# The halves of the gathered experts' weights: VectorE in place of ScalarE and GpSimd, and a two-step maximum in the routing's search

## The chip, the cores and the metric

The kernel runs on one core of a Trainium2 chip. A core has five engines that work side by side, each through its own instructions in order: PE (TensorE, matrix products), DVE (VectorE), ACT (ScalarE), POOL (GpSimd, which here also issues the gathers) and SP (which issues plain transfers). An engine that reaches an instruction whose inputs are not there stands still, and everything behind it on that engine stands too. The metric is the device time of one execution in microseconds (us), the median of three runs.

## The reference

```python
def reference(**kwargs):
    attn_out = _attn_ref(**attn_kwargs)            # 4 batches, 8 heads, 576 tokens, 64 features, window masks
    x = ...reshape(B * S, H * D)                   # 2304 tokens x 512
    x = _moe_ref(x=x, **moe_kwargs)                # greedy: each token to one expert, 288 per expert
    return _moe2_ref(x=x, **moe2_kwargs)           # every expert for every token, weights from 8 balancing rounds

# _moe_ref: logits in falling order; a token goes to the expert unless either is taken
for e in range(E):                                 # E = 8, w1[e] is 512 x 1024, w2[e] is 1024 x 512
    mask = assigned == e
    h = np.maximum(x[mask] @ w1[e], 0.0)
    out[mask] = h @ w2[e]

# _moe2_ref
for e in range(E):
    h = np.maximum(x @ w1[e], 0.0)
    out += P[:, e:e + 1] * (h @ w2[e])
```

## The kernel before

Every fp32 matrix product is made of three fp16 products: each operand is split in a high half and a low half (what the high half leaves over), and high x high, high x low and low x high are summed. So each expert's weights must be split before use. A weight piece is 128 x 1024 fp32; an expert has eight of them, four of the first layer (tiles `w1h`, `w1l`, or `w0h`, `w0l` for the first moe2 expert, whose second layer then uses the names `w1h`, `w1l`) and four of the second (`w2h`, `w2l`).

The program has three stretches: attention (to about 170 us), `stage1` (routing, moe1 and the first moe2 expert together, to about 705 us) and `stage2` (the other seven moe2 experts).

**Routing** (`Router.phase`, L511 on) closes one expert per phase, in eight phases; the phase decides which expert's weights and which tokens moe1 takes next. A phase begins with a search in six steps for a threshold. In a step VectorE compares all token maxima with 32 or 64 candidates (`G`, L548), TensorE counts them (L552, tile `r`), VectorE tests the counts (`ok`, L554), TensorE spreads the answer to all partitions (L557), and VectorE takes the largest candidate that holds (`pen`, L560 and L561), which gives `cur` and the next candidates `x` (L540). Each step needs the one before it.

**The order** is written by hand. `main` in `stage1` emits moe1's and moe2's products per phase, `interleave` puts a piece of routing between them whenever enough nanoseconds of products have been emitted (1.2 times what the piece asks for, 0.8 in phase 1), and `pump` puts a weight piece between them every few products. Nothing is reordered later: what is emitted between two routing operations stands between them on its engine. Only phase 0 has no products beside it; there the first moe2 expert's eight pieces are split, and products of no use (`warm`, L700) run.

**Weights** (`weights`, L702 on): four raw buffers. Piece n is scaled and rounded to its high half by ScalarE (L736). The low half is made in one of two ways: with `pool`, ScalarE scales the raw buffer in place (L738) and GpSimd subtracts (L739); without it, VectorE does both in one instruction (L741). Then piece n+4 is loaded into the same raw buffer. Before, `pool` holds for the first moe2 expert and for the moe1 experts of phases 1 to 7; the moe1 expert of phase 0 goes through VectorE. moe1's weights come by gathers that GpSimd issues (L761: one per piece of the first layer, two per piece of the second), since the expert is only known after the phase; the tokens' gathers (L771) stand in the same queue, and so did the subtractions. The first moe2 expert's pieces and the gate's weights (`load_gate2`) are plain loads in SP's queue.

**Hidden features**: ScalarE writes the high half `hh` (L787), VectorE the low half `hl` (L788); moe1's result goes to `x2h`, `x2l` (L821, L822).

## Time and profile before

| what | us |
|---|---|
| runs: median (lowest to highest) | 1966.06 (1960.57 to 1968.34) |
| the profiled execution: its span, first to last instruction | 1959.4 |
| median of the runs less that span | 6.7 |
| PE busy in the span | 1861.5 |
| DVE busy | 1251.1 |
| ACT busy | 853.1 |
| POOL busy | 502.7 |

The span is what the trace shows, and no time outside it is given for the profiled execution; so the span is the profiled execution's own time here. It lies 6.7 us under the runs' median and 1.2 us under their lowest. A busy PE is not a PE at its peak: the ends of products are modelled, and the granted clock can halve their pace.

### The profile page before, as it was taken

To read this page: it belongs to the slowest core of one execution; us is meant where nothing else is said; L and a number is where in the kernel's file an instruction comes from. 1 tells how busy PE (TensorE), PEld (TensorE's weight loads), DVE (VectorE), ACT (ScalarE), POOL (GpSimd) and SP (SyncE) were. 2 spreads that over 40 slices of the span, in tenths; PEclk is the share of its full clock that TensorE was granted. 3 is DMA by queue.
4 is the path that set the end of the run, shared out by engine and by line. 5 is a ranking of instruction groups with operands and counts; after the bars stand their busy time and mean duration, and the time that the engine had idled before them with its cause. 6 is when DMAs were issued, how large, how long until landed. Compare 5 with 4: busy or idle time off the path is not lost.

```text
span 1959.4 us, 35169 instructions
## 1 busy us (share of the span) xinstructions
PE 1861.5 (95%) x14812; PEld 1283.7 (66%) x14812; DVE 1251.1 (64%) x2428; ACT 853.1 (44%) x1400; POOL 502.7 (26%) x457
## 2 busy tenths in 40 slices
PE   6997699899899999999999999999999999999998
PEld 4775466665676756775776677677657766776775
DVE  5986766666631485577657765855776586658555
ACT  6775454344555332434325442424344253434332
POOL 0684565555565143011002000200110030003101
PEclk7996799999999999999999999999999999999999
DMA  9375443332344020002001100200020020001101
GB/s 218 73 152 142 109 99 88 80 78 80 70 102 137 25 65 1 1 23 65 1 1 48 40 1 1 87 1 1 23 65 1 1 65 23 1 3 42 44 2 54
DMA packets 87071, 103.47 MB, mean 53 GB/s; under 512 B 49888, under 2 KB 63968, under 8 KB 86912
## 3 DMA queue, kind: packets, MB, share of 16 engines
q1 hardware_dynamic: 73328, 57.66, 11.0%
q0 software_dynamic: 12912, 43.48, 8.5%
q8 instruction: 116, 1.90, 0.4%
q14 instruction: 43, 0.35, 0.1%
q10 hardware_dynamic: 672, 0.08, 0.0%
HBM read 88.41 MB, written 9.45 MB: 50 GB/s over the span
## 4 chain that ended last, share of the span: by engine, by line
PE 69%; DVE 16%; issue 7%; ACT 3%; DMA 2%; POOL 2%; SPq 0%; POOLq 0%; DVEq 0%; ACTq 0%
PE mm L911 26%; PE mm L944 23%; PE mm L784 7%; PE mm L818 4%; PE mm L839 4%; DVE h512l L923 2%; DVE pen L561 2%; DVE w2l L895 2%; PE r L552 1%; DVE nm L230 1%; DVE G L548 1%; DMA rawq<-in_q_dram 1%; ACT h512h L922 1%; POOL out_dram L959 1%; DVE r L918 1%
## 5 line engine op out<-in xcount | busy, mean ns | idle before, releaser
L944 PE MATMUL mm<-w2h,h512l 128*128 128x256 f16 x1568 | 427.5, 273 | 6.2 <-DVE h512l L923 5.4
L944 PE MATMUL mm<-w2h,h512h 128*128 128x256 f16 x1568 | 427.3, 273 | 3.2 <-ACT h512h L922 1.4
L944 PE MATMUL mm<-w2l,h512h 128*128 128x256 f16 x1568 | 427.3, 273 | 0.0
L911 PE MATMUL mm<-x2l,w1h 128*128 128x512 f16 (+1 forms) x1120 | 400.7, 358 | 0.0
L911 PE MATMUL mm<-x2h,w1h 128*128 128x512 f16 (+1 forms) x1120 | 400.7, 358 | 0.0
L911 PE MATMUL mm<-x2h,w1l 128*128 128x512 f16 (+1 forms) x1120 | 400.7, 358 | 0.0
L911 PEld LDWEIGHTS <-w1h 128*128 128x128 f16 x2240 | 219.2, 98 | 210.1
L944 PEld LDWEIGHTS <-h512h 128*128 128x128 f16 x3136 | 306.2, 98 | 48.7 <-issue 5.6
L914 ACT ACTIVATE r<-mm 128x512 f32<-128x512 f32 (+1 forms) x280 | 151.9, 546 | 333.4 <-PE mm L911 333.4
L885 POOL TENSOR_TENSOR raw<-raw 128x256 f32<-128x256 f32 x28 | 22.4, 799 | 998.9 <-DMA raw<-in_w2b_dram 950.5
L911 PEld LDWEIGHTS <-w1l 128*128 128x128 f16 x1120 | 109.6, 98 | 108.2
L922 ACT ACTIVATE h512h<-r 128x1024 f16<-128x1024 f32 x112 | 118.4, 1057 | 133.4 <-DVE r L918 133.4
L944 PEld LDWEIGHTS <-h512l 128*128 128x128 f16 x1568 | 153.3, 98 | 27.2 <-DVE h512l L923 9.5
L917 DVE TENSOR_TENSOR S<-r 128x256 f32<-128x256 f32 (+1 forms) x140 | 56.3, 402 | 176.6 <-ACT r L914 174.9
L923 DVE TENSOR_TENSOR h512l<-r,h512h 128x1024 f16<-128x1024 f32 x112 | 143.3, 1279 | 38.2 <-ACT h512h L922 38.1
L788 DVE SCALAR_TENSOR_TENSOR hl<-mm,hh 128x288 f16<-128x288 f32 (+2 forms) x128 | 55.5, 452 | 88.4 <-ACT hh L787 86.8
L923 DVE TENSOR_TENSOR h512l<-S,h512h 128x768 f16<-128x768 f32 x112 | 110.7, 988 | 0.0
L787 ACT ACTIVATE hh<-mm 128x288 f16<-128x288 f32 (+2 forms) x128 | 50.4, 405 | 115.2 <-PE mm L784 114.1
L955 DVE SCALAR_TENSOR_TENSOR acc<-t,P,acc 128x512 f32<-128x512 f32 x126 | 97.3, 772 | 5.1
L784 PE MATMUL mm<-xt,w1h 128*128 128x288 f16 x512 | 98.2, 292 | 2.1 <-ACT xt L801 2.1
L969 DVE TENSOR_TENSOR t<-mm,t 128x256 f32<-128x256 f32 x63 | 26.7, 424 | 107.3 <-ACT t L968 107.3
L922 ACT ACTIVATE h512h<-S 128x768 f16<-128x768 f32 x112 | 92.9, 829 | 5.1 <-DVE S L920 4.6
(254 smaller groups left out, 3516.1 us busy)
## 6 DMA issues: line engine op xcount, KB each, us to landing
raw<-in_w1b_dram SPq DMA_DIRECT2D x32, 512.0 KB, 4.5
raw<-in_w2b_dram SPq DMA_DIRECT2D x32, 512.0 KB, 3.7
rawv<-in_v_dram SPq DMA_DIRECT2D x36, 128.0 KB, 2.8
xd<-xo SPq DMA_DIRECT2D x29, 96.0 KB, 2.0
xd<-rpk SPq DMA_DIRECT2D x11, 96.0 KB, 2.1
rawk<-in_k_dram SPq DMA_DIRECT2D x1, 1024.0 KB
rawq<-in_q_dram SPq DMA_DIRECT2D x1, 1024.0 KB
raw<-in_w2a_dram,widx POOLq DMA_INDIRECT x64
```

Of the source, the lines that this page charges most:

```text
L784: nc.tensor.matmul(p, a[:, k, 128 * f:128 * (f + 1)], rhs(k, b), start=(k == 0 and i == 0), stop=(k == KT - 1 and i == 2))
L787: nc.scalar.activation(h[0][:, f, :n], p, AF.Relu)
L788: nc.vector.scalar_tensor_tensor(h[1][:, f, :n], p, 0.0, h[0][:, f, :n], op0=OP.max, op1=OP.subtract)
L818: nc.tensor.matmul(p, a[:, f, c], b[:, f, :CAP], start=(f == 0 and i == 0), stop=(f == FT - 1 and i == 2))
L839: nc.tensor.matmul(p, a[:, f, c], b[:, f, :], start=(f == 0 and j == 0), stop=(f == FT - 1 and j == 2))
L911: nc.tensor.matmul(p, a[:, k, 128 * f:128 * (f + 1)], self.x2[b][:, k, t0:t0 + n], start=(k == 0 and j == 0), stop=(k == KT - 1 and j == 2))
L914: nc.scalar.activation(c[:, s], p.rearrange("p (s t) -> p s t", s=2), AF.Relu, scale=SH)
L917: V.tensor_add(S[:, 0], a21, a22)
L922: nc.scalar.activation(hq[0][:, i, s, :m], x, AF.Copy)
L923: V.tensor_sub(hq[1][:, i, s, :m], x, hq[0][:, i, s, :m])
L944: nc.tensor.matmul(p, h[u][:, i, a, 128 * i0:128 * (i0 + 1)], w[v][:, i, b, :], start=(q in (1, 7) and i == 0 and j == 0), stop=(q in (2, ...
L955: V.scalar_tensor_tensor(self.acc[:, r, :], x, self.P[:, r, e:e + 1], self.acc[:, r, :], op0=OP.mult, op1=OP.add)
```

## The change

The low halves of the eight pieces of the first moe2 expert, and of the 56 pieces of moe1's experts of phases 1 to 7, are no longer made by a scaling on ScalarE and a subtraction on GpSimd but by one instruction on VectorE, as those of phase 0's expert already were. In the routing's search, one custom VectorE instruction that adds, takes the maximum and accumulates it (it leaves a second instruction that reads the accumulator) becomes a plain addition and a plain maximum over the row. Comments and blank lines aside, that is all; lines behind the split move up by 5, and the new maximum is L562.

```diff
@@ Router.phase
                 V.tensor_scalar(pen, q[:, :T], 0.5, -3e38, op0=OP.is_lt, op1=OP.mult)
-                V.tensor_tensor_reduce(out=pen, in0=pen, in1=c, scale=1.0, scalar=-3e38, op0=OP.add, op1=OP.max,
-                                       accum_out=cur)
+                V.tensor_add(pen, pen, c)
+                V.tensor_reduce(cur, pen, axis=AX.X, op=OP.max)
@@ Moe.weights
-    def weights(self, key, letter, fetch, pool):
+    def weights(self, key, letter, fetch):
...
             nc.scalar.activation(hi, r, AF.Copy, scale=sc[lay])
-            if pool:
-                nc.scalar.activation(r, r, AF.Copy, scale=sc[lay])
-                nc.gpsimd.tensor_sub(lo, r, hi)
-            else:
-                nc.vector.scalar_tensor_tensor(lo, r, sc[lay], hi, op0=OP.mult, op1=OP.subtract)
+            nc.vector.scalar_tensor_tensor(lo, r, sc[lay], hi, op0=OP.mult, op1=OP.subtract)
@@ Moe.stage1
-        w0 = self.weights(("b", 0), "a", self.fetch_static(0), True)
+        w0 = self.weights(("b", 0), "a", self.fetch_static(0))
...
-            w = self.weights(("a", ph), "b", self.fetch_gather(ph), ph > 0)
+            w = self.weights(("a", ph), "b", self.fetch_gather(ph))
```

The first place is VectorE in the search of phase 2, steps three and four. Before, two steps stand there like this:

```order
L554 TENSOR_SCALAR ok<-r,rem 8x32
L560 TENSOR_SCALAR pen<-r 128x32
L561 ISA pen,cur<-pen,x 128x32
L561 ISA cur 128x1
L540 TENSOR_TENSOR x<-thr,cur 128x32
L548 TENSOR_TENSOR G<-m,x 128x288 x2
```

Now the same steps read:

```order
L554 TENSOR_SCALAR ok<-r,rem 8x32
L736 SCALAR_TENSOR_TENSOR w2l<-raw,w2h 128x1024
L560 TENSOR_SCALAR pen<-r 128x32
L561 TENSOR_TENSOR pen<-pen,x 128x32
L562 TENSOR_REDUCE cur<-pen 128x1
L540 TENSOR_TENSOR x<-thr,cur 128x32
L548 TENSOR_TENSOR G<-m,x 128x288 x2
L736 SCALAR_TENSOR_TENSOR w2l<-raw,w2h 128x1024
L554 TENSOR_SCALAR ok<-r,rem 8x32
L736 SCALAR_TENSOR_TENSOR w2l<-raw,w2h 128x1024
```

The low half of a second-layer piece has come between `ok` and `pen`, or between `G` and `ok`, and the custom pair (ISA) is now an addition and a maximum.

The second place is GpSimd's queue over one moe1 expert (phase 2's), from its first gathers to those of the next expert. Before:

```order
L761 DMA raw<-in_w1a_dram,widx 128x1024 x4
L771 DMA xg<-xd,idx 96x1024 x3
L739 TENSOR_TENSOR w1l<-raw,w1h 128x1024
L761 DMA raw<-in_w2a_dram,widx 128x512 x2
...
L739 TENSOR_TENSOR w2l<-raw,w2h 128x1024 x4
L761 DMA raw<-in_w1a_dram,widx 128x1024 x4
```

Now:

```order
L756 DMA raw<-in_w1a_dram,widx 128x1024 x4
L766 DMA xg<-xd,idx 96x1024 x3
L756 DMA raw<-in_w2a_dram,widx 128x512 x8
L756 DMA raw<-in_w1a_dram,widx 128x1024 x4
L766 DMA xg<-xd,idx 96x1024 x3
```

The eight subtractions have left the queue, and only gathers stand in it; a gather into a raw buffer now waits for VectorE's instruction on that buffer.

The third place is VectorE at the end of phase 0, where the first moe1 expert's token list `idx` is made. Before:

```order
L634 SCALAR_TENSOR_TENSOR mask<-zv,mask 128x18
L635 TENSOR_TENSOR L<-L,ng 128x144
L643 COPY s_3660<-r 96x6
L644 SCALAR_TENSOR_TENSOR idx<-s_3660 96x3
L527 TENSOR_REDUCE m<-L 128x18
```

Now:

```order
L635 TENSOR_TENSOR L<-L,ng 128x144
L736 SCALAR_TENSOR_TENSOR w1l<-raw,w1h 128x1024
L643 COPY s_3659<-r 96x6
L644 SCALAR_TENSOR_TENSOR idx<-s_3659 96x3
L736 SCALAR_TENSOR_TENSOR w1l<-raw,w1h 128x1024
L527 TENSOR_REDUCE m<-L 128x18
```

The last two pieces of the first moe2 expert now stand around `idx`, and free the raw buffers that the last two of the first four gathers need.

## Rows read from the trace of the kernel before

**Rows 1.** The page: busy time by engine; the chain that ended last, by line.
```profile
PE 1861.5 (95%) x14812; PEld 1283.7 (66%) x14812; DVE 1251.1 (64%) x2428; ACT 853.1 (44%) x1400; POOL 502.7 (26%) x457
PE mm L911 26%; PE mm L944 23%; PE mm L784 7%; PE mm L818 4%; PE mm L839 4%; DVE h512l L923 2%; DVE pen L561 2%; DVE w2l L895 2%; PE r L552 1%; DVE nm L230 1%; DVE G L548 1%; DMA rawq<-in_q_dram 1%; ACT h512h L922 1%; POOL out_dram L959 1%; DVE r L918 1%
```

**Rows 3.** Groups by line, 165 to 640: busy us, mean ns; idle before.
```profile
L738 ACT ACTIVATE raw<-raw 128x1024 f32<-128x1024 f32 x64 | 67.6, 1057 | 5.6
...
L561 DVE CUSTOM_DVE_ANT_0 pen<-pen,x 128x32 f32<-128x32 f32 x28 | 46.2, 1651 | 1.0
L741 DVE SCALAR_TENSOR_TENSOR w2l<-raw,w2h 128x1024 f16<-128x1024 f32 x4 | 4.9, 1222 | 2.9 <-issue 2.1 <-ACT w2h L736 0.8
L561 DVE DVE_READ_ACCUMULATOR2_ANT cur<- 128x1 f32 x42 | 3.3, 79 | 0.0
L609 DVE TENSOR_TENSOR pos<-pos,r 128x36 f32<-128x36 f32 x8 | 1.5, 192 | 0.3
L582 DVE TENSOR_REDUCE wx<-r 128x1 f32<-128x8 f32 x7 | 1.1, 164 | 3.7 <-PE r L580 3.7
```

**Rows 4.** Timeline of DVE and of POOL, 283 to 345: start, us, instruction.
```profile
290.44 5.49 DVE L561 CUSTOM_DVE_ANT_0 pen<-pen,x 128x32 f32<-128x32 f32 x1
...
287.51 8.37 POOL L739 TENSOR_TENSOR w2l<-raw,w2h 128x1024 f16<-128x1024 f32 x4
```

**Rows 5.** PE's waits, 165 to 720: total us, times, longest us.
```profile
PE r L552 <- DVE G L548: 33.7, 13, 5.3
PE mm L839 <- ACT hh L787: 2.7, 2, 2.4
```

**Rows 6.** Waits of all engines, 262 to 640.
```profile
PE r L552 <- DVE G L548: 21.2, 8, 5.3
ACT w2h L736 <- DMA raw<-in_w2a_dram,widx: 17.8, 13, 3.4
```

**Rows 7.** Waits of all engines, 229 to 262.
```profile
PE r L552 <- DVE G L548: 0.2, 1, 0.2
```

**Rows 8.** Windows from PE's restart behind four waits for L548.
```profile
353.22:358.00 4.78, 4.78 (x39) 3.08 (x39) 2.05 (x9) 0.41 (x1) 0.00 (x0) 0.64 0.00 0
410.44:416.00 5.56, 5.56 (x45) 3.66 (x45) 2.88 (x9) 0.82 (x2) 0.00 (x0) 0.69 0.00 0
467.70:474.00 6.30, 6.29 (x35) 2.50 (x35) 2.60 (x8) 0.00 (x0) 0.00 (x0) 0.59 0.01 3
526.42:532.00 5.58, 5.58 (x36) 2.73 (x36) 3.75 (x12) 0.38 (x1) 0.00 (x0) 0.59 0.01 1
```

**Rows 9.** Windows of stage 1: length; busy us (count) by engine, clock, DMA share, GB/s.
```profile
165.00:225.00 60.00, 39.49 (x355) 20.39 (x353) 39.95 (x101) 25.01 (x30) 28.84 (x18) 0.60 0.45 128
229.00:262.00 33.00, 30.36 (x320) 22.57 (x319) 23.73 (x79) 8.62 (x16) 8.55 (x8) 1.00 0.29 90
262.00:560.00 298.00, 274.21 (x2550) 189.52 (x2548) 188.67 (x515) 137.97 (x206) 164.99 (x119) 0.97 0.35 86
```

**Rows 10.** The chain in order of time, 500 to 720: start, us, what.
```profile
620.63 2.14 POOL w1l L739
...
624.31 3.48 DMA raw<-in_w2a_dram,widx
627.87 1.06 ACT w2h L736
```

**Rows 11.** Timeline of DVE and of POOL, 165 to 285.
```profile
219.90 3.48 DVE L741 SCALAR_TENSOR_TENSOR w1l<-raw,w1h 128x1024 f16<-128x1024 f32 x3
...
215.17 0.93 POOL L771 DMA_INDIRECT xg<-xd,idx  x1 [0.72 <-DVE idx L644]
...
221.37 2.85 POOL L761 DMA_INDIRECT raw<-in_w2a_dram,widx  x1 [2.50 <-DVE w1l L741]
224.52 0.96 POOL L761 DMA_INDIRECT raw<-in_w2a_dram,widx  x1 [0.30 <-issue]
```

## The prediction

> **What bounds the kernel now.** The page first. TensorE is busy 95% of the span, and the chain that ended last runs mostly through its products; but one line that is no product stands high in it, the routing's `pen` on VectorE (L561, 2%, so about 40 us of 1959.4) [rows 1]. It is an instruction on 32 or 64 numbers per partition and should be too small to be seen. Look next at its durations: half of them are 225 ns or less, the longest is 7582 ns [rows 2]. The group of 28 has 46.2 us where 28 of the shortest, 0.191, would have 5.3 [rows 2, 3]; some 41 us are standing still inside the instruction.

> The timeline says on whom. One starts at 290.44 and lasts 5.49 us, to 295.93; GpSimd ran four subtractions of `w2l` back to back from 287.51 for 8.37 us, to 295.88 [rows 4]. VectorE was held until GpSimd's last subtraction was over. Whichever of the two makes it so, the custom instruction or the subtraction, both go: all of GpSimd's subtractions in this stretch come from the line (L739) that the change removes.

> Then the waits, for what this costs TensorE. Between 165 and 720 us TensorE's largest wait is for `G` (L548), the work right behind `pen`: 33.7 us in 13 waits [rows 5]. 21.2 us in 8 of them lie in 262 to 640, where moe1 and moe2 run beside the routing [rows 6], 0.2 us in 229 to 262 [rows 7], and the rest, 33.7 - 21.2 - 0.2 = 12.3 us, in phase 0, where TensorE has only products of no use to do, so that there VectorE's own chain counts and not TensorE's wait. [...] So in stage 1 what ends last is a VectorE that GpSimd holds; in stage 2, two thirds of the span, nothing of the change runs.

> **The change, part by part.**

> *The waits for G go.* With L739 gone GpSimd issues only gathers there. Take 21.2 us [rows 6].

> *The clock behind them.* What a window loses is its length times what is missing from 1: 4.78 x 0.36 = 1.7, 5.56 x 0.31 = 1.7, 6.30 x 0.41 = 2.6, 5.58 x 0.41 = 2.3, together 8.3 us [rows 8]. TensorE waited for `G` just ahead of each and was busy through all of each, so without the waits I expect the clock to stay. Bounds: 0 if something else makes it fall, 8.3 if not. I take 8.3.

> *The late weights.* Where no routing runs any more, a piece comes late: a subtraction on GpSimd from 620.63 for 2.14 us, behind it the gather of the next piece, 3.48 us from 624.31, then ScalarE's high half at 627.87 [rows 10], and `hh` queued behind that on ScalarE makes TensorE wait 2.7 us in two waits [rows 5]. Now the buffer is free after VectorE's 1.22 us in place of 1.06 (L738) and 2.14, and each queue of gathers loses eight subtractions. Take 2.6 of the 2.7.

> *VectorE's new work.* 64 instructions at 1.22 us [rows 3] are 78 us, of which 56 (68 us) lie beside the products. VectorE was busy 188.7 of 298 us in 262 to 560 [rows 9], about 41 of it standing still. Some 45 of the pieces fall in there: 188.7 - 41 + 55 = 203 of roughly 270 us, or 75%. Whether that can be borne is answered by a stretch that already works in the new way: from 229 to 262 VectorE splits four `w2l` pieces of phase 0's expert (L741) between the steps of phase 1's search, is busy 23.7 of 33 us, 72% [rows 9], and TensorE waits 0.2 us for `G` [rows 7]. By that row 56 pieces cost 56 x 0.2 / 4 = 2.8 us; I take 3. The other end is each piece fully exposed, 68 us; the row of the same operations between the same steps is the nearer one, so I stay by it. What covers a piece is the products that stand between one step's answer and the next count; if a piece stands where they don't reach, up to 1.22 us is seen, and `ok`, `pen` and `hl` are queued behind it.

> *ScalarE's work that goes.* 67.6 us of scaling [rows 3]. ScalarE is no bound, but `hh` stood behind it; I count nothing, and this is the reason why I don't count more for the line above.

> *Addition and maximum.* 0.19 (L609) + 0.16 (L582) in place of 0.19 (the shortest L561) + 0.08 (the accumulator's read) [rows 2, 3]: 0.1 us more a step, at most 0.2 with the gaps. 36 steps are hidden behind the products between the steps; without that cover they would be 4 to 7 us. The six of phase 0 are counted there.

> *Phase 0* has no cover. VectorE wins about 11 us of standing (the 12.3 us of TensorE's waits, less about 1 us for the comparisons themselves). It pays 8 x 1.22 = 9.8 us of splits, about 1 us for addition and maximum, and up to two splits, 2.4 us, for the gate's weights, whose load stands in SP's queue behind loads into buffers that VectorE now frees; some 2 to 3 us of all this lie behind TensorE's answers (an estimate: a quarter to a third of each split, since TensorE needs a few tenths to answer). So about 0. But the last two pieces free their raw buffers only around `idx`, the first four gathers of moe1's weights wait for those buffers, and the tokens' gathers, which began at 215.17 [rows 11], wait behind them. Two of the four gathers can start only after the splits at the end: I put the start of moe1 1 us later (0 to 3).

> *The gathers beside VectorE's split.* A gather's issue took 0.96 us, but 2.85 us when it fell under VectorE's three splits from 219.90 on [rows 11]. So each of an expert's 12 gathers of weights may be up to 1.9 us slower to issue; but GpSimd's queue loses eight subtractions of 2.14, 17 us an expert, and the row of TensorE's waits in 229 to 262 holds such gathers already. I count 0. [...]

> **Sum.** 21.2 + 8.3 + 2.6 - 3 - 1 = 28.1 us less than the profiled execution's 1959.4, so a span of 1931. The median of the runs is 6.7 us above that span; the same step down from it gives 1966.1 - 28.1 = **1938 us**.

> **The rivals.** (What a measurement of this kernel can tell from no change is about 0.5%, 9.8 us.)

> *VectorE is late instead.* If an eighth to a quarter of the 68 us is exposed (8 to 17 us), and a wait of the old kind with a low clock behind it comes back once or twice (1.7 to 2.6 each), the gain is 10 to 20: 1946 to 1956. For it speak the places where two splits stand with only `ok` between them ahead of the next answer (2.44 us where the old order had none); against it the 0.2 us of [rows 7].

> *VectorE takes all of it back*: nearly half of the 68 exposed, within 9.8 us of 1966. Against it the same row.

> *Slower: the weights' gathers hold VectorE.* ScalarE already stands for the second layer's gathers, 17.8 us in 13 waits, 1.4 each [rows 6]. Until now only ScalarE stood; now VectorE's low half waits for ScalarE's high half, and the search behind it. If each of the 28 gathered second-layer pieces of phases 1 to 7 is exposed so (28 x 1.4 = 39 us) and four low clocks come back (8.3), the waits are 47 against 32 won: 1966 + 15 = 1981. It decides from about 1.1 us a piece (32 / 28). Against it: the gathers come sooner, since no subtraction stands before them, and the four pieces between 229 and 262 did not do it.

> *More than thought*: VectorE stood some 41 us and TensorE waited only half of that; if the search running earlier also removes waits that are put down to others, another 5 to 8 us: 1930.

> *The change doesn't do what it says*, that is the waits come from something else than the subtraction: the end of the held instruction at 295.93 beside 295.88 makes that unlikely, and both partners go at once; it is in the second rival's chance.

> **Numbers.** Likeliest (gain 20 to 36, 1930 to 1946): 0.62. More: 0.06. VectorE late, gain 10 to 20: 0.17. All taken back: 0.09. Slower: 0.06. Faster by over 0.5%: 0.62 + 0.06 + 0.17 = 0.85; within: 0.09; slower: 0.06. The range for 8 in 10 takes the likeliest, a part of the more, and nearly all of the second: 1927 to 1955.

> **What the next profile would show.** Right: the new addition at about 0.2 us with no long ones; no subtraction in stage 1; TensorE's wait for `G` in 229 to 640 down from 21.4 to a few us; a granted clock of 1.00 there; VectorE at about 75% between 262 and the end of the routing; stage 2 unchanged and only shifted. Wrong: waits for `G` or `ok` behind a split, a VectorE wait for `w2h`, or low clocks at new places. Phase 0 is right if moe1's first product starts within 3 us of where it did.

## The result, and the profile of the changed kernel

The change takes the median from 1967.20 to **1938.39 us** (four runs of each; 1936.58 to 1941.52 against 1960.57 to 1972.14): a ratio of 0.9862, with a 95% interval of 0.9843 to 0.9881 (ratios here are worked out from all the runs; the quotient of the two medians would be 0.9854). Forecast were 1938 and 1927 to 1955. The two profiled executions lie closer together, with spans of 1959.4 and 1939.7, since before's was one of the short ones of its kernel and this is the longest of the four of the changed one (1941.5). What follows from that comes below; first the changed kernel's own views.

The page: busy time by engine, and the chain that ended last by line.

```profile
PE 1859.8 (96%) x14812; PEld 1286.3 (66%) x14812; DVE 1274.3 (66%) x2492; ACT 787.6 (41%) x1336; POOL 373.2 (19%) x393
PE mm L906 26%; PE mm L939 23%; PE mm L779 10%; PE mm L813 4%; PE mm L834 4%; DVE h512l L918 2%; DVE w2l L890 2%; PE r L552 1%; DVE nm L230 1%; DMA rawq<-in_q_dram 1%; DVE ptl L256 1%; DVE r L913 1%; ACT h512h L917 1%; POOL out_dram L954 1%; DVE vh L198 1%
```

Below line 735 names stand five lines earlier than before: moe1's products are L779 (were L784), the split is L736 (was L741). `pen`, which had 2% of the chain [rows 1], is no longer among its lines here. GpSimd has 129.5 us less, ScalarE 65.5 less, VectorE 23.2 more: 64 splits of 1.22 are 78, and over 50 of standing still went.

VectorE's groups by line, 165 to 640 (busy us, mean ns; idle time before them and what ended it):

```profile
L736 DVE SCALAR_TENSOR_TENSOR w1l<-raw,w1h 128x1024 f16<-128x1024 f32 x36 | 43.9, 1221 | 12.6 <-ACT w1h L735 10.9 <-issue 1.0 <-DMA raw<-in_w2a_dram,widx 0.5
L736 DVE SCALAR_TENSOR_TENSOR w2l<-raw,w2h 128x1024 f16<-128x1024 f32 x32 | 39.0, 1220 | 18.3 <-ACT w2h L735 17.2 <-PE mm L779 0.5 <-issue 0.4
L561 DVE TENSOR_TENSOR pen<-pen,x 128x32 f32<-128x32 f32 x28 | 5.4, 192 | 1.0
```

The durations of the addition and of the maximum over the whole run (min/median/max in ns):

```profile
L561 DVE TENSOR_TENSOR pen<-pen,x x35: 191/193/226, 183.8 to 520.1; 128x32 f32<-128x32 f32 x28, 128x64 f32<-128x64 f32 x7
L562 DVE TENSOR_REDUCE cur<-pen x42: 185/186/221, 179.7 to 520.3; 128x1 f32<-128x32 f32 x28, 128x1 f32<-128x64 f32 x14
```

The group of 28 that had 46.2 us [rows 3] has 5.4, and its longest instruction takes 226 ns where it took 7582 [rows 2]. Nothing stands still inside an instruction of the search now: `x` takes 226 ns at most and `G` 759, where they took up to 2080 and 3032. New is VectorE's own wait of 17.2 us for ScalarE's high half of `w2`.

TensorE's waits, 229 to 640 (us in total, times, longest).

```profile
PE mm L779 <- DVE x2l L817: 4.3, 3, 2.4
PE r L557 <- DVE ok L554: 3.3, 5, 1.2
PE r L552 <- issue: 2.3, 3, 1.2
PE mm L779 <- ACT xt L796: 0.9, 1, 0.9
PE r L552 <- DVE G L548: 0.4, 1, 0.4
```

The wait for `G` fell from 21.2 + 0.2 [rows 6, 7] to 0.4, and the 2.7 us for a late `hh` [rows 5] are gone. In their place stand 3.3 us for `ok` (0.9 before), which is queued behind a split.

Windows: length, busy us (count) of TensorE, its weight loads, VectorE, ScalarE and GpSimd, granted clock, DMA share, GB/s. First of the changed kernel:

```profile
229.00:262.00 33.00, 32.26 (x318) 23.18 (x317) 22.59 (x74) 8.53 (x16) 5.41 (x7) 0.93 0.18 50
262.00:560.00 298.00, 287.91 (x2695) 202.62 (x2695) 203.99 (x574) 103.03 (x177) 95.73 (x88) 0.98 0.42 97
226.94:233.76 6.82, 5.70 (x44) 3.53 (x44) 3.71 (x10) 2.90 (x4) 4.00 (x4) 0.50 0.79 223
264.48:271.31 6.83, 6.83 (x46) 5.28 (x44) 3.83 (x12) 1.16 (x4) 2.16 (x2) 0.50 0.72 124
340.00:560.00 220.00, 215.84 (x2032) 151.22 (x2031) 151.66 (x431) 76.51 (x131) 70.86 (x64) 1.00 0.41 95
```

and of the kernel before, for two of these stretches:

```profile
226.94:233.76 6.82, 4.86 (x52) 3.62 (x52) 4.30 (x12) 3.49 (x6) 5.30 (x6) 1.00 0.70 209
340.00:560.00 220.00, 200.25 (x1820) 136.38 (x1818) 140.37 (x381) 95.73 (x145) 116.98 (x84) 0.95 0.33 82
```

From 340 on the clock is 1.00 where it was 0.95, and TensorE is busy 215.8 of 220 us where it was 200.3. But two stretches of 6.8 us at a granted clock of 0.50 stand in moe1's first 45 us, where the profile of before has none. What 0.50 does to the products shows in a third, short stretch of the changed kernel, from 336.16 to 339.57: those of 128x512 start 0.41 to 0.43 us apart there, and 0.21 to 0.22 apart from 339.69 on. In this one pair of profiles the clock therefore gave nearly nothing, about 7 us of clock lost early against the four windows won. Whether the change makes the new ones is a question for the experiments.

### The profile page after: what moved, and what is told of

Read it like the earlier page. It is cut to its first block, busy times and chain, and to the rows that moved or that the text cites. A ratio compares the mean times of both kernels' runs of the same rounds, so it can differ in the third digit from the quotient of the medians.

```text
span 1939.7 us, 35063 instructions
## 1 busy us (share of the span) xinstructions
PE 1859.8 (96%) x14812; PEld 1286.3 (66%) x14812; DVE 1274.3 (66%) x2492; ACT 787.6 (41%) x1336; POOL 373.2 (19%) x393
## 4 chain that ended last, share of the span: by engine, by line
PE 72%; DVE 14%; issue 7%; ACT 3%; DMA 2%; POOL 1%; SPq 0%; POOLq 0%; DVEq 0%; ACTq 0%
PE mm L906 26%; PE mm L939 23%; PE mm L779 10%; PE mm L813 4%; PE mm L834 4%; DVE h512l L918 2%; DVE w2l L890 2%; PE r L552 1%; DVE nm L230 1%; DMA rawq<-in_q_dram 1%; DVE ptl L256 1%; DVE r L913 1%; ACT h512h L917 1%; POOL out_dram L954 1%; DVE vh L198 1%
## 5 line engine op out<-in xcount | busy, mean ns | idle before, releaser
L912 DVE TENSOR_TENSOR S<-r 128x256 f32<-128x256 f32 (+1 forms) x140 | 56.2, 402 | 176.2 <-ACT r L909 174.6
L779 PE MATMUL mm<-xt,w1h 128*128 128x288 f16 x512 | 97.4, 290 | 0.9 <-ACT xt L796 0.9
```

The source lines that it names most:

```text
L779: nc.tensor.matmul(p, a[:, k, 128 * f:128 * (f + 1)], rhs(k, b), start=(k == 0 and i == 0), stop=(k == KT - 1 and i == 2))
L912: V.tensor_add(S[:, 0], a21, a22)
```

## The experiments

Where an expectation names a theory by a letter, it is one of these. Theory H (holding): VectorE's instructions with two inputs in SBUF stand until GpSimd's subtractions are over; the gain is the end of that, by way of the split alone, and the plainer search gains nothing by itself. Its sharper form, R (reading): only GpSimd instructions that read SBUF hold VectorE (R2 is its other half: only VectorE's instructions with two SBUF inputs are held). The rivals: the custom instruction of the search is all that gets held (C), so that addition and maximum would win by themselves; addition and maximum bring a part of their own (A); VectorE's instructions are held whatever they read (any); the weights are ready sooner (W), or ScalarE's 68 us of relief is the gain; any work on GpSimd would do the harm (B), for instance by making the gathers late. Ratios are to the kernel before on the same chip, whose medians there were 1968.37, 1970.12 and 1968.55; line numbers shift by a few with each edit.

**The split alone.** The custom instruction stays.

```diff
-                V.tensor_add(pen, pen, c)
-                V.tensor_reduce(cur, pen, axis=AX.X, op=OP.max)
+                V.tensor_tensor_reduce(out=pen, in0=pen, in1=c, scale=1.0, scalar=-3e38, op0=OP.add, op1=OP.max,
+                                       accum_out=cur)
```

> Only the split goes to VectorE; the search keeps its custom instruction. Theory H (VectorE is held by GpSimd's subtractions, whatever instruction it has): all of the gain, 1938 within 5 us, no custom instruction over 0.5 us beside the products. Theory C (only the custom instruction can be held): the same, since nothing is left that holds it. Theory A (the plain addition and maximum bring a part of their own): 1945 or more.

1934.53; ratio 0.9832 (0.9811 to 0.9853). The whole gain is there. The durations of the custom instruction in this kernel:

```profile
L561 DVE CUSTOM_DVE_ANT_0 pen<-pen,x x35: 191/192/228, 184.9 to 513.8; 128x32 f32<-128x32 f32 x28, 128x64 f32<-128x64 f32 x7
```

Its longest is 228 ns against 7582 [rows 2], so nothing in the instruction itself is slow.

**Addition and maximum alone.** The kernel before with the search alone changed; the weights are split as before, by ScalarE's scaling and GpSimd's subtraction. Against the kernel before:

```diff
-                V.tensor_tensor_reduce(out=pen, in0=pen, in1=c, scale=1.0, scalar=-3e38, op0=OP.add, op1=OP.max,
-                                       accum_out=cur)
+                V.tensor_add(pen, pen, c)
+                V.tensor_reduce(cur, pen, axis=AX.X, op=OP.max)
```

> Only the addition and the maximum are put in; the split stays with ScalarE and GpSimd. Theory H: no gain, 1967 within 8 us; the standing moves to the addition, to x or to G, and TensorE's waits for G between 262 and 640 stay at 15 us or more. Theory C: most of the gain, 1940 within 6. Theory A: some gain, 1945 to 1960.

1969.67; ratio 1.0007 (0.9994 to 1.0019): no change. The plain addition is held as the custom instruction was. Durations of the two lines:

```profile
L561 DVE TENSOR_TENSOR pen<-pen,x x35: 191/224/7968, 185.1 to 548.9; 128x32 f32<-128x32 f32 x28, 128x64 f32<-128x64 f32 x7
L562 DVE TENSOR_REDUCE cur<-pen x42: 185/186/221, 182.1 to 549.1; 128x1 f32<-128x32 f32 x28, 128x1 f32<-128x64 f32 x14
```

Rows of the timeline of GpSimd and of VectorE (start, us):

```profile
296.20 8.38 POOL L739 TENSOR_TENSOR w2l<-raw,w2h 128x1024 f16<-128x1024 f32 x4
299.36 5.28 DVE L561 TENSOR_TENSOR pen<-pen,x 128x32 f32<-128x32 f32 x1
304.67 0.19 DVE L562 TENSOR_REDUCE cur<-pen 128x1 f32<-128x32 f32 x1
```

GpSimd's four subtractions end at 304.58, the addition at 304.64. The maximum, with one input, is never held here: 221 ns at most, against 7968 for the addition with both inputs in SBUF.

This kernel has all the holding of before, and its profile (span 1971.2) has the low clock at moe1's start as well. Two of its windows:

```profile
232.24:239.07 6.83, 5.90 (x40) 3.37 (x40) 3.04 (x8) 2.30 (x4) 3.37 (x3) 0.50 0.69 229
269.78:276.61 6.83, 6.83 (x46) 5.32 (x44) 4.21 (x13) 1.89 (x4) 3.06 (x3) 0.50 0.65 77
```

So those two stretches don't come from the split's new place. The profile of before happened to be without them, and its mean granted clock, 0.973, is above that of each of the 31 other executions of that kernel beside the experiments (0.962 to 0.972).

**One input out of SBUF.** The kernel before, with its custom instruction cut in two and the penalty left in PSUM, so that the addition reads SBUF only once.

```diff
-                V.tensor_scalar(pen, q[:, :T], 0.5, -3e38, op0=OP.is_lt, op1=OP.mult)
-                V.tensor_tensor_reduce(out=pen, in0=pen, in1=c, scale=1.0, scalar=-3e38, op0=OP.add, op1=OP.max,
-                                       accum_out=cur)
+                V.tensor_scalar(q[:, :T], q[:, :T], 0.5, -3e38, op0=OP.is_lt, op1=OP.mult)
+                V.tensor_add(pen, q[:, :T], c)
+                V.tensor_reduce(cur, pen, axis=AX.X, op=OP.max)
```

> The split stays with ScalarE and GpSimd as before; the search adds with one operand from PSUM (the penalty is written there), so that the addition reads SBUF once. Theory R2 (held are instructions with two SBUF inputs): no addition over 0.5 us, but x and G, which have two, take the standing over, and TensorE's waits for G stay at 15 us or more: 1968 within 8. Theory any: the additions are held as before, up to 8 us.

One execution, 1965.84, span 1964.0. Durations of the addition and of the next instruction with two SBUF inputs, the `x` of L540:

```profile
L561 DVE TENSOR_TENSOR pen<-r,x x35: 190/191/225, 184.8 to 541.9; 128x32 f32<-128x32 f32 x28, 128x64 f32<-128x64 f32 x7
L540 DVE TENSOR_TENSOR x<-thr,cur x35: 191/224/7510, 181.8 to 535.5; 128x32 int32<-128x32 int32 x28, 128x64 int32<-128x64 int32 x7
```

Rows of the timeline of GpSimd and of VectorE:

```profile
291.55 6.29 POOL L739 TENSOR_TENSOR w2l<-raw,w2h 128x1024 f16<-128x1024 f32 x3
...
293.72 0.19 DVE L561 TENSOR_TENSOR pen<-r,x 128x32 f32<-128x32 f32 x1
294.17 3.73 DVE L540 TENSOR_TENSOR x<-thr,cur 128x32 int32<-128x32 int32 x1
```

TensorE's largest wait, 262 to 640:

```profile
PE r L552 <- DVE G L548: 21.5, 9, 5.1
```

The addition ran through in 0.19 us in the midst of GpSimd's run (291.55 to 297.84), and the next instruction but one was held until 297.90 in its place. What is held is decided here by the inputs (225 ns at most with one in SBUF, 7510 with two); TensorE's waits for `G` are the same 21.5 us, since the step has another such instruction behind it.

The five traces with such subtractions in 165 to 640 us (before, addition and maximum alone, this one, and two further down: GpSimd reads again, the first expert on GpSimd) agree one by one. Of VectorE's instructions that began with at least 0.7 us of a subtraction still to run, the 83 with two tensors in SBUF all ended after the subtraction, and the 168 with at most one all ended in their usual time. Two more, with one tensor and a scalar per partition (`cur`) from SBUF, were held as well, one here and one with the addition and maximum alone, whose durations are:

```profile
L564 DVE TENSOR_SCALAR G<-m,cur x7: 242/243/1744, 208.2 to 549.4; 128x18 f16<-128x18 f32 x7
```

Whether the scalar counts as the second input there is not shown.

**GpSimd reads again.** The changed kernel, with a subtraction on GpSimd for every piece ahead of VectorE's split. Its result lands in a tile that nobody reads.

```diff
+            nc.gpsimd.tensor_sub(self.junk.rearrange("p (a b) -> p a b", a=per), r, hi)
             nc.vector.scalar_tensor_tensor(lo, r, sc[lay], hi, op0=OP.mult, op1=OP.subtract)
```

> The change, and on GpSimd again a subtraction per piece of the size of the old one, into a tile that nobody reads (the result is the reference's). Theory H: the gain is lost again, 1958 to 1972, with long instructions on VectorE at the addition, x or G and TensorE's waits for G between 262 and 640 back to 12 us or more. Theory C: 1938 within 5. Theory W (the gain came from the weights being ready sooner on ScalarE and GpSimd): 1941 to 1950, without long instructions on VectorE.

2025.70; ratio 1.0294 (1.0272 to 1.0317), far beyond the kernel before. Durations of the addition, and VectorE's groups by line, 165 to 640:

```profile
L561 DVE TENSOR_TENSOR pen<-pen,x x35: 191/193/2394, 188.6 to 592.9; 128x32 f32<-128x32 f32 x28, 128x64 f32<-128x64 f32 x7
...
L737 DVE SCALAR_TENSOR_TENSOR w1l<-raw,w1h 128x1024 f16<-128x1024 f32 x32 | 58.4, 1828 | 7.9 <-ACT w1h L735 7.9
L737 DVE SCALAR_TENSOR_TENSOR w2l<-raw,w2h 128x1024 f16<-128x1024 f32 x27 | 56.4, 2091 | 8.1 <-ACT w2h L735 8.1
L548 DVE TENSOR_TENSOR G<-m,x 128x288 f16<-128x288 f32 x56 | 51.4, 958 | 1.0
...
L784 DVE SCALAR_TENSOR_TENSOR hl<-mm,hh 128x288 f16<-128x288 f32 x48 | 20.7, 450 | 12.0 <-ACT hh L783 11.9
```

TensorE's two largest waits, 262 to 640:

```profile
PE r L557 <- DVE ok L554: 23.2, 13, 5.1
PE r L552 <- DVE G L548: 19.5, 15, 3.8
```

Theory H has the direction, and its size was too small: it left out that VectorE's own split has two inputs in SBUF and is held too (1.83 and 2.09 us against 1.22), with `ok` queued behind it. `hl` has one input in PSUM and keeps its time (450 ns on average; 454 in the changed kernel). Against the changed kernel the span grew by 84.5. TensorE's waits from 225 to 640 grew from 15.6 to 64.2, that is by 48.6; moe1's first work on TensorE, the transposes of its tokens, started at 238.66 where it had been 225.46. Of the rest, some 23 us, 7 are waits for `hl` and `hh` between 640 and 720, and what is left fits the low clocks: between 238 and 640 stretches at 0.50 sum to 58.0 us, against 17.1 in the changed kernel between 225 and 640, which at half clock is at most 20.5 us more.

**GpSimd writes only.** The same place, two fills of the unread tile, which read nothing.

```diff
+            for _ in range(2):
+                nc.gpsimd.memset(self.junk, 0.0)
             nc.vector.scalar_tensor_tensor(lo, r, sc[lay], hi, op0=OP.mult, op1=OP.subtract)
```

> The change, and on GpSimd two fills of a tile that nobody reads per piece: work that writes SBUF and reads nothing. Theory R (VectorE is held by what GpSimd reads): as the change, 1940 within 5, no long instruction on VectorE. Theory B (any GpSimd work holds it): slower by 10 us or more, with long additions, x or G as under the subtractions.

1945.21; ratio 0.9878 (0.9858 to 0.9898); the split alone, on the same chip at the same time, had 1936.27. Durations of the fills and of the addition:

```profile
L737 POOL MEMSET junk<- x144: 941/951/977, 178.3 to 618.2; 128x1024 f16 x144
L561 DVE TENSOR_TENSOR pen<-pen,x x35: 191/192/226, 185.0 to 524.8; 128x32 f32<-128x32 f32 x28, 128x64 f32<-128x64 f32 x7
```

Rows of the timeline of ScalarE, VectorE and TensorE (start, us; in brackets the idle time before and what ended it):

```profile
399.59 1.06 ACT L735 ACTIVATE w2h<-raw 128x1024 f16<-128x1024 f32 x1 [3.33 <-DMA raw<-in_w2a_dram,widx]
...
400.68 1.22 DVE L738 SCALAR_TENSOR_TENSOR w2l<-raw,w2h 128x1024 f16<-128x1024 f32 x1 [3.16 <-ACT w2h L735]
401.82 0.23 DVE L554 TENSOR_SCALAR ok<-r,rem 8x32 f16<-8x32 f32 x1
...
402.11 0.17 PE L557 MATMUL r<-ok,ones 8*128 8x32 f16 x1 [4.84 <-DVE ok L554]
```

GpSimd is busy nearly as long as with its subtractions (2 x 0.95 us a piece against 2.1), and VectorE's search and splits are not held: the addition takes 226 ns at most here against 2394 under the dummy subtractions, `G` 759 against 3140, and the splits 1.22 us on average against 1.83 and 2.09. That is theory R, though the time lies 0.2 us outside the range that R was given. The 9 us that the fills cost over the split alone show the *slower* rival of the prediction on a small scale: the gather comes late, ScalarE waits 3.33 us for it, VectorE 3.16 for ScalarE, `ok` is queued behind, and TensorE waits 4.84. In the changed kernel that chain is there too (17.2 us of VectorE's waiting for `w2h`), but TensorE sees no more than 1.2 us of it at once. So of the 32 us by which the split alone lies under the kernel before here, some 23 stay when GpSimd is kept busy without reading SBUF, and some 9 hang on its queue being free for the gathers.

**The first expert on GpSimd.** The change, with the first moe2 expert's eight pieces left where they were. Against the kernel before, beside the addition and maximum as above:

```diff
-            w = self.weights(("a", ph), "b", self.fetch_gather(ph), ph > 0)
+            w = self.weights(("a", ph), "b", self.fetch_gather(ph), False)
```

> As the change, but the eight pieces of the first moe2 expert, in phase 0, stay with ScalarE and GpSimd. My sum has about 0 in phase 0 and a start of moe1 later by 0 to 3 us: so 1937 within 4, with moe1's first product within 2 us of its place in the change. If phase 0 gained more than I put down (the 11 us of standing weigh more than the splits): 1943 or more.

1936.70; ratio 0.9848 (0.9829 to 0.9867): as the change. Phase 0, from its first comparison to the first transposes of moe1's tokens, took 51.1 us here (178.3 to 229.39), 49.3 in the changed kernel (176.2 to 225.46), 49.4 in before (175.8 to 225.22). What phase 0 wins or pays is at most 2 us in these profiles, and the time doesn't show it.

**ScalarE's scaling put back,** as a dummy beside the change.

```diff
+            nc.scalar.activation(self.junk.rearrange("p (a b) -> p a b", a=per), r, AF.Copy, scale=sc[lay])
```

> The change, and on ScalarE again a scaling of each of the 64 pieces (1.05 us), into a tile that nobody reads. My sum counted nothing for ScalarE's relief: within 4 us of the change. Rival: the relief is a real part of the gain, 8 us or more slower than the change, with TensorE waiting for hh or VectorE for w2h.

1940.73; ratio 0.9845 (0.9822 to 0.9868); the change, beside it, 1943.66. ScalarE's relief is worth nothing that can be measured.

**The change and the split once more.**

> The change once more, beside the split alone on the same chip. If the addition and maximum cost what the rows say (0.1 to 0.2 us a step, covered by products): no difference to the split alone beyond 2 us. If they cost what the first comparison seemed to show: the change is 3 to 5 us slower, with a wait of TensorE for the next count that the profile puts down to nothing, near 334 us.

> The split alone once more: 1935 within 3 us; if the addition and maximum cost nothing, within 2 us of the change in the same runs.

1943.66 (0.9847; 0.9822 to 0.9873) and 1939.79 (0.9845; 0.9822 to 0.9869). The split alone missed its 1935 within 3, and the medians lie 3.9 us apart, which is within the 3 to 5 us of the second forecast. But the executions overlap over nearly all their length (1937.87 to 1945.81 and 1937.22 to 1945.27), and the ratios and their intervals coincide: the addition and the maximum neither win nor cost what five runs can tell. The 2.3 us of "issue" ahead of `r` in the changed kernel's profile are not in its second one, so they don't belong to every execution of it.

**More warming.** Two runs tried for more than the change gives. In the first, the split alone, TensorE does 32 products of no use instead of 16 while it waits for the first expert's tokens.

```diff
-        self.warm(16)
+        self.warm(32)
```

> The split alone, with 32 products of no use in place of 16 ahead of moe1's first tokens. If the low clock behind the wait for the tokens' gather (226 to 233 us in the change) comes from that idle stretch: the granted clock is 1.00 in 225 to 262 and the time falls by 3 to 5 us. If not, or if the products now stand in the way: no gain, or up to 2 us more.

1942.44; ratio 0.9848 (0.9825 to 0.9870), no gain. TensorE doesn't wait for the tokens any more (3.5 us in the changed kernel), but for their transposed copy `xt` instead, and its clock still falls to 0.50 twice. The first fall is half as long, the second stays. The wait just ahead of the first fall (in 225 to 262) and the windows, columns as above:

```profile
PE mm L779 <- ACT xt L796: 2.9, 1, 2.9
...
230.79:234.20 3.41, 3.41 (x32) 1.99 (x31) 1.94 (x4) 0.41 (x1) 0.38 (x1) 0.50 0.57 149
264.93:271.76 6.83, 6.83 (x46) 5.30 (x44) 4.46 (x14) 1.71 (x3) 3.07 (x3) 0.50 0.64 72
```

So the idle time ahead of the first fall was moved and not taken away, and the run can't tell whether the fall comes from it. In the profile of the kernel with the first expert on GpSimd there is one such stretch, of 3.4 us. The second fall stands behind a wait of 2.4 us for `x2l` at 264; the profile of before has that wait too, at 261.83, and its clock is 1.00 behind it. So the wait alone doesn't explain that fall, and the cause of both stays open.

**More room in front of the routing's runs.** The split alone, with the factor on the products that the interleaving leaves ahead of each run of the search in phase 1 raised from 0.8 to 1.05; beside it the split alone a third time.

```diff
-EARLY, SLACK, SL2 = 2, 0.8, 1.2
+EARLY, SLACK, SL2 = 2, 1.05, 1.2
```

> The split alone, and the pieces of phase 1's routing asked for later (1.05 in place of 0.8 of their time), which puts the fourth x2l of the first moe1 expert ahead of the routing's tail on VectorE. If the wait for x2l at 264 us (2.4 us) and the low clock behind it (264 to 271) hang on that order: both go, 3 to 6 us less than the split alone. Rival: the wait only moves to the next phase, within 2 us of the split alone.

> The split alone, as the measure for the run beside it: 1937 within 5 us.

1944.69 (0.9869; 0.9847 to 0.9892) against 1936.27 (0.9832; 0.9814 to 0.9849): worse, if anything. At 264 both went, as expected: no wait for `x2l` stands there, and the clock is 1.00 in the window below. But the wait only moved, as in the rival: 2.4 us of it stand at 324, with a low stretch of 3.4 us behind them, and another low stretch of 3.4 us stands at 283. In sum the wait for `x2l` fell by 1.2 us, and a split that stood for ScalarE brought a new wait. The window, and rows of the timeline of VectorE and TensorE:

```profile
264.00:272.00 8.00, 8.00 (x87) 7.26 (x85) 7.62 (x25) 2.41 (x7) 3.69 (x4) 1.00 0.78 231
...
563.67 1.23 DVE L736 SCALAR_TENSOR_TENSOR w2l<-raw,w2h 128x1024 f16<-128x1024 f32 x1 [4.30 <-ACT w2h L735]
...
565.28 0.27 PE L779 MATMUL mm<-x2h,w0h 128*128 128x256 f16 x1 [3.33 <-DVE hl L783]
```

No version is clearly better than the change; those with the custom instruction kept are its equal.

## Why the prediction was right

*The holding.* Right, and shown from four sides: it ends with the split alone (the custom instruction's longest is 228 ns), it stays with the addition alone (7968), it moves to the next two-input instruction when the addition gets an input from PSUM (225 for the addition, 7510 for `x`), and it returns with a dummy subtraction (2394) but not with a fill (226). The two candidates that the prediction left side by side, custom instruction or subtraction, are told apart: it is the subtraction.

*The waits for `G`*: 21.2 forecast; 21.4 fell to 0.4. *The late weights*: 2.6 forecast; the 2.7 us for `hh` are gone.

*The clock*: 8.3 forecast, and in the pair of profiles not borne out: at most about 2, and the mean over 229 to 640 is 0.98 in both. From 340 on the clock is whole again, as forecast. The small net gain comes from the two stretches at moe1's start, which a kernel that still has all the holding shows too. Against that kernel (addition alone), as the like one, the forecast is within reach. It has five low stretches around its waits for `G`, 27.3 us long together, from 307 to 543; the changed kernel has one of 3.4 us in all that time, at 336. At half clock, with half the products' pace as above, that is at most (27.3 - 3.4) x 0.5 = 12 us. What the term is in a usual pair of executions stays open.

*VectorE's new work*: 3 forecast; the wait for `ok` was 3.3, and 1.6 to 5.4 in the other profiles with the split on VectorE and nothing new on GpSimd. VectorE was forecast to be busy 203 of some 270 us, 75%; it was 204.0 us in 262 to 560, but those are 298 us, so 68%. The row of 229 to 262 [rows 7] was a good model of the rest.

*Start of moe1*: 1 us later forecast; the first transposes come 0.2 later, the first product at 228.88 where it was 228.90, and phase 0 up to the transposes is 0.2 shorter. That sum hides two parts, of which the prediction had put the first at about 0 and named the second. Phase 0's chain did get shorter: its products of no use ahead of the transposes began 42.9 us after the first comparison before, 40.3 now. But the tokens were not there sooner, so TensorE waited 4.1 us for them where it had waited 0.4. *ScalarE's relief*, *addition and maximum*: 0 forecast; the experiments that isolate them agree within the spread of the runs (the medians of the addition and maximum alone lie 1.3 us above before, those of the change 3.9 above the split alone). *The gathers*: 0 forecast; an issue of a second-layer gather takes 1.13 us on average between 165 and 640 where it took 1.03, and TensorE's waits above show no part of that by itself.

*The sum.* 28.1 us forecast; the medians differ by 28.8 in the first comparison, by 26.5 in the second, by 30 to 34 with the split alone. The agreement to half a microsecond is partly luck, since the executions of one kernel spread over 3 to 13 us. The profiled spans differ by 19.7 alone, a short execution against a long one, and the span forecast, 1931, was missed by 8.7. What the profiles do show adds up. TensorE's waits from 225 to 640 went from 31.5 to 15.6; that is 21.0 for `G` and 2.7 for `hh`, against 3.7 more for the first tokens' transposes, 2.4 for `ok`, 2.4 for issue, and -0.7 in the others. The low clock gives about 2 more. That is 18, and from the first transposes to the end of moe1 and moe2's first expert the two profiles differ by 19.4 (478.85 against 459.45).

*The rivals.* VectorE late, taken back, slower: none came at its size. But of the signs that the prediction named for being wrong, three are there, and small: 3.3 us of waits for `ok` behind a split, VectorE's wait for `w2h`, and low clocks at new places. And the slower rival's mechanism is real. It shows when the gathers are delayed (the fills: TensorE waits 4.84 us at once) or the order shifts (more room: 3.33).

## What to carry to other kernels

A tiny instruction with a long maximum next to a short median (7582 ns and 225 [rows 2]) was being held here. Look at what ends in the same tenth of a microsecond on the neighbouring engine (295.93 and 295.88 [rows 4]), and count the inputs that each of the two reads from SBUF: in these traces the 83 with two tensors were held, the 168 with at most one were not, and two with a tensor and a scalar per partition were (one of them for 1744 ns in place of 243). Moving work from GpSimd to the engine that waited for it paid here (ratio 0.9832 for the split alone) although that engine got fuller (1274.3 us busy in place of 1251.1), since its new work fits under products that are there anyway; a stretch of the old kernel that already worked in the new way gave the price (2.8 us for 56 pieces; the wait for `ok` came to 3.3). Making one held instruction immune gained nothing (TensorE's waits for `G` were 21.5 us with it and 21.2 without), since the next one has two such inputs as well; and a profiled step should be set against the spread of executions before a term is called right or wrong.

## What the runs showed that was not expected

An instruction of 0.19 us stood through several of GpSimd's subtractions in a row, each a separate instruction of about 2.1 us, up to 7.97 us: it did not get in between two of them. The wait went to the end of a whole run of subtractions, where each follows the one before without a gap (in the profile of before, each of a run starts 28 to 56 ns ahead of the end of the one before it). Where a gap stands between them it did get in: under the dummy subtractions three run from 253.97 to 256.10, 256.18 to 258.30 and 258.38 to 260.82; the addition ended behind the first, and `x`, the next instruction but one, behind the second:

```profile
253.97 6.85 POOL L736 TENSOR_TENSOR junk<-raw,w2h 128x1024 f16<-128x1024 f32 x3
...
254.12 2.04 DVE L561 TENSOR_TENSOR pen<-pen,x 128x32 f32<-128x32 f32 x1
256.19 0.19 DVE L562 TENSOR_REDUCE cur<-pen 128x1 f32<-128x32 f32 x1
256.42 1.93 DVE L540 TENSOR_TENSOR x<-thr,cur 128x32 int32<-128x32 int32 x1
```

The gap is 0.08 us, and in that trace no addition and no `x` stood through one.

Held as one of the pair, a large instruction paid as well: VectorE's split of 128 x 1024 went from 1.22 to 1.83 and 2.09 us on average beside GpSimd's subtraction of the same piece, and that subtraction from 2.17 and 2.13 to 2.26 and 2.42 (first and second layer).

The gathers paid beside VectorE's split: in the changed kernel the 29 whose issue lay for over 0.5 us beside a split took 1.45 us on average and up to 2.40, the 93 that met none 0.99. The 2.85 us of [rows 11] were no single case.
